# Weight decode sums on VectorE, copies of turned probabilities on ScalarE, in a decay-attention and low-rank MLP kernel

## The chip, the cores and the metric

The kernel runs on one core of one Trainium2 chip. The metric is the device time of an execution in microseconds; the median of several runs is compared. The core has five engines that run side by side and meet at semaphores: TensorE (PE, with its weight loads PEld), VectorE (DVE), ScalarE (ACT), GpSimd (POOL) and SyncE (SP), which here issues nearly all DMAs.

## The reference

Attention over 8 batches x 8 heads, 576 tokens, head size 64, with a causal decay, and then a token mix of rank 32 and a channel MLP on the result:

```python
scores = scale * np.matmul(q, k.transpose(0, 1, 3, 2))
log_f = np.log(np.clip(f, 0.0001, 1.0))
cum = np.cumsum(log_f, axis=-1)
decay = cum[:, :, :, None] - cum[:, :, None, :]
scores = np.where(causal, -1000000000.0, scores + decay)
attn = np.exp(scores - np.max(scores, axis=-1, keepdims=True))
attn = attn / (np.sum(attn, axis=-1, keepdims=True) + 1e-09)
x = heads_to_columns(np.matmul(attn, v))
h = x.transpose(0, 2, 1) @ U @ V
u = x + h.transpose(0, 2, 1)
return u + np.maximum(u @ w_ch1, 0.0) @ w_ch2
```

`w_ch1` is 512 x 2048, `w_ch2` 2048 x 512. U, V and both matrices reach the chip as 64-bit floating-point numbers.

## The kernel before

**Steps and pairs.** The 64 heads are worked on as 32 pairs (four to a batch). A step (`step(t)`) has ten slots. It computes the scores of pair t (S for the four main row blocks of both heads, St for the 64-token tail), turns the probabilities of pair t−1 over on TensorE (T, T_v, Ty) and multiplies them with the values: head 0 of pair t−1 in slot 7 of step t, head 1 in slot 0 of step t+1 (V). Behind that come the rank-32 product (Tt), and after every fourth pair the mix (H, Tu, Tv) and the first part of the MLP (A, B), slipped in between the slots. A score block goes: S on TensorE into a PSUM bank; a row maximum with the mask on VectorE (L365, L391 for the tail), which writes nm; the exponential on ScalarE (L373, L401), which writes P and frees the bank. Each V group ends with its evacuation to xn on VectorE (L520 and L525), which frees the one V area of PSUM that T_v uses too.

**The first six pairs** (p < NF = 6) work in plain float32: the turned probabilities are copied once out of PSUM. `evac` records that copy. In `turn_p` the groups 0 and 2 of each head are copied by ScalarE and group 1 (128x384) by VectorE; in `turn_tail` the two halves of the turned tail (128x256 each) by VectorE. From the seventh pair on (p >= 6) the operands are split into a high and a low part: ScalarE copies the high part (L422), VectorE subtracts to get the low one (L423), whatever engine `evac` was given. Of these pairs GpSimd builds the split operands G of the scores (L309 on POOL, L322, L323), and it also makes the low part of xn for the rank-32 product in every step (L595, L596).

**The weight decode.** Before the seventh pair, fourteen weight units are brought from 64-bit numbers into a high part (h) and a low part (l): units 0, 1, 3, 4, 6, 7 are chunks of w1, unit 2 is U, unit 5 is V, units 8 to 13 are chunks of w2. Each is loaded by SyncE into a staging tile (`load_w`; stg for w1, U, V; a part of the third xn buffer and stg for w2) two or three units ahead, and decoded (`decode_w`, `decode`) at places in the steps that the list DECODES gives: two to three units a step from step 0 to 5, the last in step 7. One decode is eight instructions on one tile: a scaling on ScalarE (L60), bit work on VectorE (L65, L66, L67, L68), the sum of the two parts (L69), the rounding copy to h on ScalarE (L70) and the subtraction that leaves l (L71). L69 and L71 are on `sub`, which is GpSimd for all fourteen units. Each waits for the one ahead of it. A second decode, of the remaining weights at about 710 to 810 us, has `sub=nc.vector` already and is not touched.

**What sets the order.** TensorE's order is written out by hand in the whole attention part. In step 0, and from step 7 on, SyncE's is too. The orders of VectorE, ScalarE and GpSimd (in steps 1 to 6 SyncE's as well) are made by the scheduler when the program is built, so a change of engine reorders what stands around it; pins (`keep_in_program_order`) hold only each decode's first instruction, the w2 loads and the clearing of G. Every engine works its queue strictly in order.

Of the kernel before, what the change touches and what calls it, by code (L numbers as in the profile page):

```python
# [21 lines left out]
P = 128  # L22
# [18 lines left out]
def tile_decay_attention_moe(ctx, tc, qk, v, f, U, V, w1, w2, out):  # L41
    nc = tc.nc
# [8 lines left out]
    def decode(raw, a, h, l, eng, rows=slice(0, 128), keep=False, sub=nc.gpsimd):  # L51

        lo, hi = raw[..., 0].bitcast(U32), raw[..., 1]
        af, gf = a.bitcast(F32), hi.bitcast(F32)
        if eng is nc.scalar:
            first = nc.scalar.mul(af, gf, 2.0**-112)  # L60
        else:
            first = eng.tensor_scalar(af, gf, 2.0**-112, None, op0=ALU.mult)
        if keep:
            tc.keep_in_program_order(first)
        nc.vector.tensor_scalar(hi, hi, -0x80000000, None, op0=ALU.bitwise_and)  # L65
        nc.vector.scalar_tensor_tensor(a, a, 3, hi, op0=ALU.logical_shift_left, op1=ALU.bitwise_or)  # L66
        nc.vector.tensor_scalar(hi, a, -0x800000, None, op0=ALU.bitwise_and)  # L67
        nc.vector.scalar_tensor_tensor(gf, lo, 2.0**-52, gf, op0=ALU.mult, op1=ALU.mult)  # L68
        sub.tensor_tensor(af, af, gf, op=ALU.add)  # L69
        nc.scalar.copy(h, af)  # L70
        sub.tensor_tensor(l[rows], af[rows], h.bitcast(F32)[rows], op=ALU.subtract)  # L71
# [126 lines left out]
    def load_w(u):  # L198
        if u in staged or u >= len(UNITS):
            return  # L200
        kind, fc = UNITS[u]
        n = {"U": (NM + 1) * RK, "V": S}.get(kind, 512)
        if kind == "w2":

            spare = xn[NX - 1].rearrange("p c d -> p (c d)").bitcast(I32)
            if fc % 2:
                raw, a = spare[:, 1536:2560], sb.tile([P, 512], I32, tag="w2a", name=f"stg{u}")
            else:
                raw, a = spare[:, 0:1024], spare[:, 1024:1536]
        else:  # L210
            t = sf.tile([P, 3 * S], I32, tag=("uh", "ul", "hh", "hl")[u % 4], name=f"stg{u}")
            raw, a = t[:, 0 : 2 * n], t[:, 2 * n : 3 * n]
        staged[u] = raw.rearrange("p (n t) -> p n t", t=2), a
        if kind == "w1":
            nc.sync.dma_start(raw, w1_src(fc))
        elif kind == "w2":
            tc.keep_in_program_order(nc.sync.dma_start(raw, w2_src(fc)))
        elif kind == "V":
            for g in range(4):
                nc.sync.dma_start(raw[32 * g : 32 * g + 32], words(V))  # L220
        else:
            r4 = raw.rearrange("p (c r) -> p c r", c=NM + 1)
            nc.sync.dma_start(r4[:, 0:NM], words(U[0:MAIN]).rearrange("(c p) r -> p c r", p=P))
            for g in range(2):
                nc.sync.dma_start(r4[64 * g : 64 * g + 64, NM], words(U[MAIN:S]))

    def decode_w(u):
        load_w(u)
        raw, a = staged.pop(u)
        staged[u] = None  # L230
        kind, fc = UNITS[u]
        if kind == "w1":
            h, l = (x[:, fc].rearrange("p c f -> p (c f)") for x in (w1h, w1l))
        elif kind == "w2":
            h, l = w2h[:, fc], w2l[:, fc]
        elif kind == "V":
            h, l = VV, VV
        else:
            raw = raw.rearrange("p (c r) t -> p c r t", c=NM + 1)
            a = a.rearrange("p (c r) -> p c r", c=NM + 1)  # L240
            h, l = Us[:, :, 0:RK], Us[:, :, RK : 2 * RK]
        decode(raw, a, h, l, nc.scalar, slice(96, 128) if kind == "V" else slice(0, 128), keep=True)
        if u == len(UNITS) - 1:
            nc.gpsimd.memset(xn[NX - 1][64:128, NM, :], 0.0)

# [7 lines left out]
    def defer(phase, fn, slots=1):  # L253
        later.setdefault(now[0] + slots, []).append((phase, fn))
# [53 lines left out]
    def copy(eng, dst, src):  # L308
        return eng.copy(dst, src) if eng is nc.scalar else eng.tensor_copy(dst, src)  # L309
# [105 lines left out]
        nc.vector.reciprocal(z["rv"][:, 0:9], sm[:, 0:9])  # L415
        nc.vector.tensor_copy(z["rv"][0:64, 9:10], z["rv"][64:128, 8:9])

    def evac(dsth, dstl, src, eng=nc.scalar):
        if dstl is None:
            defer(0, lambda: copy(eng, dsth, src))  # L420
            return
        defer(0, lambda: nc.scalar.copy(dsth, src))  # L422
        defer(2, lambda: nc.vector.tensor_tensor(dstl, src, dsth.bitcast(F32), op=ALU.subtract))  # L423

    GRP = (((0, 0), (0, 1), (0, 2), (0, 3)), ((1, 1), (1, 2), (1, 3)), ((2, 2), (2, 3), (3, 3)))
# [1 line left out]
    def turn_p(p, j, g):  # L427
        z = st[p]
        if "PTh" not in z:
            kind = F32 if p < NF else F32R  # L430
            z["PTh"] = sb.tile([P, 2, PTW], kind, tag="PTh", name=f"PTh{p}")
            z["PTl"] = sb.tile([P, 2, PTW], F32R, tag="PTl", name=f"PTl{p}") if p >= NF else None
            z["PT4"] = sb.tile([P, P], kind, tag="PT4", name=f"PT4{p}")
        grp = GRP[g]
        if (j, g) == (0, 2):
            z["tv"] = psV.tile([P, 1024], F32, tag="V", name=f"T{p}_v")
            tp = z["tv"][:, 0:512]
        else:
            tp = psT.tile([P, 512], F32, tag="T", name=f"T{p}_{j}{g}")
        for x, (c, i) in enumerate(grp):  # L440
            nc.tensor.transpose(tp[:, P * x : P * x + P], z["P"][j][i][:, P * c : P * c + P], ident)  # L441

        x = 0
        for c in sorted({c for c, _ in grp}):
            m = sum(1 for cc, _ in grp if cc == c)
            sl = slice(OC[c], OC[c] + P * m)
            low = z["PTl"][:, j, sl] if p >= NF else None
            evac(z["PTh"][:, j, sl], low, tp[:, P * x : P * (x + m)], nc.vector if g == 1 else nc.scalar)
            x += m

    def turn_tail(p):
        z = st[p]
        tp = z["tv"][:, 512:1024]
        for c in range(NM):
            nc.tensor.transpose(tp[:, P * c : P * c + P], z["ptl"][:, P * c : P * c + P], ident)

        tpv = tp.rearrange("p (c j t) -> p j c t", c=NM, j=2)
        for c in range(0, NM, 2):
            o = [(OC[c + y] + MAIN - P * (c + y)) // TAIL for y in range(2)]
            pair = [  # L460
                z[n] and z[n].rearrange("p j (y d) -> p j y d", d=TAIL)[:, :, o[0] : o[1] + 1 : o[1] - o[0]]
                for n in ("PTh", "PTl")
            ]
            evac(pair[0], pair[1], tpv[:, :, c : c + 2], nc.vector)

    def turn_small(pa, px):

# [284 lines left out]
    with tc.manual_schedule(engines=None):  # L752
# [30 lines left out]
        stream(bare, 26)  # L783
        load_w(3)
    decode_w(0)
    mixing = []
    DECODES = [(0, 2), (0, 5), (0, 8), (1, 2), (1, 7), (2, 3), (2, 8), (3, 6), (4, 2), (4, 6), (5, 2), (5, 6), (7, 1)]
# [6 lines left out]
    def step(t):  # L794
# [11 lines left out]
        for s in range(6 + 2 if last else SLOTS):  # L806
# [20 lines left out]
            if (t, s) in DECODES:  # L827
                u = 1 + DECODES.index((t, s))

                steps = [lambda: load_w(u + (3 if u < 6 else 2)), lambda: decode_w(u)]  # L830
                for fn in steps if u < 8 else steps[::-1]:
                    at(6, fn)
# [21 lines left out]
            if pa and s < 3:  # L854
                turn_p(a, 0, s)
# [4 lines left out]
            if pa and s == 5:  # L860
                turn_tail(a)
            if pa and 6 <= s < 9:
                turn_p(a, 1, s - 6)
# [110 lines left out]
    def first(g, u, i):  # L974

        ps = psF.tile([P, 512], F32, tag="F", name=f"Hb{g}_{i}")
        m = 0
        for c in range(NDC):
            for wt_, ut in ((b1h, u[0]), (b1l, u[0]), (b1h, u[1])):
                nc.tensor.matmul(ps, wt_[i][:, c], ut[:, c, 0:MAIN], start=m == 0, stop=m == 3 * NDC - 1)  # L980
                m += 1
        h = hidden(f"{g}_{i}")
        relu(h, ps, slice(0, MAIN))
        return h
# [25 lines left out]
    for i in range(NB // 2):  # L1010
        blocks = []
        for x in range(3):
            if i < 3:
                pair = [hm[:, i, 2 * P * x : 2 * P * x + 2 * P] for hm in homes]
            else:
                k = 6 * (i - 3) + 2 * x
                pair = [more[y // 4][:, 256 * (y % 4) : 256 * (y % 4) + 256] for y in (k, k + 1)]
# [114 lines left out]
    u = cur  # L1132
    ready = []
    with tc.manual_schedule(engines={ET.PE}):
        for n, g in enumerate(order):
# [4 lines left out]
            z = {"g": g, "acc": acc, "po": [None] * NM, "done": [0] * NM}  # L1140
            if n == 0:
                for i in range(NB):
                    h = first(g, u, i)
# [17 lines left out]
            u = un  # L1161
# [50 lines left out]
```

## Time and profile before

| | |
|---|---|
| median of 3 runs | 1255.39 us (1253.97 to 1256.29) |
| the profiled execution's own time | 1257.95 us |
| its span, first to last instruction | 1256.2 us |
| mean granted TensorE clock | 0.989 |
| busy PE / DVE / ACT / POOL | 97% / 69% / 51% / 36% |
| DMA | 125.87 MB, 100 GB/s over the span |

Busy times come from one execution taken by the hardware profiler. A row of a timeline gives the start in us, the time in us, engine, line, operation, tiles (written <- read), their size and a count, and in brackets how long the engine stood idle before it and what released it; "issue" means that the profile shows no releaser. A row of a group gives the least, median and largest time of one instruction in ns and the first and last start. A row of the stage table gives the stage, its length, the busy time of PE, PEld, DVE, ACT and POOL with instruction counts, the granted clock of TensorE (1.00 is full), the share of the DMA engines and GB/s. TensorE's float32 matmuls are recorded as more than one instruction, so counts there are larger than in the program.

### The profile page before, as it was taken

Reading aid. Unit: us, or ns where it says so; the run is one execution under the profiler, and the core shown is the slowest. Engines: PE = TensorE matmul, PEld = TensorE weight load, DVE = VectorE, ACT = ScalarE, POOL = GpSimd, SP = SyncE. Lnnn points to the kernel's source line nnn. Section 1 sums busy time; section 2 is a strip of 40 time slices with the busy share of each in tenths; the row PEclk is TensorE's granted clock in tenths of the full one; section 3 lists DMA queues with packets and bytes.
Section 4 is the critical chain, followed back from the end, with each engine's and each line's share of the span. In section 5 each row is a group of like instructions: output and inputs, shape, how many; then the busy total and the mean of one; then the engine's idle time right before and its main releaser. Section 6 shows DMA issues by size and latency. Waiting matters only on the chain.

```text
span 1256.2 us, 21878 instructions
## 1 busy us (share of the span) xinstructions
PE 1215.8 (97%) x7824; PEld 1074.1 (86%) x7824; DVE 866.6 (69%) x2193; ACT 638.5 (51%) x1717; POOL 456.3 (36%) x403
## 2 busy tenths in 40 slices
PE   8898899999999999999999999989999999999998
PEld 4676798998988998989989888878888888888887
DVE  8776778767778668777777699884554645556453
ACT  5565677867777767778666443332121221212211
POOL 5445455534444444545342000342331513315100
PEclk9798999999999999999999999999999999999999
DMA  7533332632434425326322256110221303213010
GB/s 178 132 106 108 113 104 71 182 96 76 140 94 149 118 75 167 85 71 179 98 74 89 92 175 253 34 68 29 106 85 51 135 9 127 79 56 134 2 34 34
DMA packets 67580, 125.87 MB, mean 100 GB/s; under 512 B 7408, under 2 KB 31984, under 8 KB 65424
## 3 DMA queue, kind: packets, MB, share of 16 engines
q1 hardware_dynamic: 67408, 124.47, 32.4%
q8 instruction: 62, 1.02, 0.4%
q14 instruction: 46, 0.38, 0.1%
q10 hardware_dynamic: 64, 0.00, 0.0%
HBM read 88.65 MB, written 35.78 MB: 99 GB/s over the span
## 4 chain that ended last, share of the span: by engine, by line
PE 81%; DVE 8%; ACT 6%; issue 3%; DMA 2%; SPq 0%; POOL 0%; ACTq 0%; DVEq 0%; POOLq 0%
PE O L994 20%; PE M L1070 16%; PE A L701 10%; PE B L719 9%; PE V L544 5%; PE T L441 3%; PE S L344 3%; PE Hb L980 2%; PE V L516 2%; PE S L345 2%; ACT G L309 1%; ACT P L373 1%; PE Tt L610 1%; PE St L344 1%; PE S L341 1%
## 5 line engine op out<-in xcount | busy, mean ns | idle before, releaser
L1093 DVE TENSOR_TENSOR sum<-M,sum 128x256 f32<-128x256 f32 x280 | 117.6, 422 | 172.2 <-PE M L1070 171.2
L971 ACT ACTIVATE bh<-sum 128x256 fp32r<-128x256 f32 x160 | 66.3, 418 | 258.6 <-DVE sum L1093 258.6
L373 ACT ACTIVATE P<-S,nm 128x128 f32<-128x128 f32 (+3 forms) x256 | 137.3, 537 | 64.8 <-DVE nm L365 52.6
L365 DVE CUSTOM_DVE_ANT_0 S<-S,mask 128x128 f32<-128x128 f32 (+3 forms) x256 | 125.7, 495 | 55.9 <-PE S L345 45.8
L994 PE MATMUL O<-b2h,bh 128*128 128x512 f32 x360 | 142.9, 397 | 0.0
L994 PE MATMUL O<-b2l,bh 128*128 128x512 f32 x360 | 142.2, 395 | 0.0
L994 PE MATMUL O<-b2h,bl 128*128 128x512 f32 x360 | 141.7, 394 | 0.0
L309 POOL CAST G<-qk 64x576 fp32r<-64x576 f32 x52 | 34.6, 666 | 250.3 <-PE St L345 150.8
L701 PE MATMUL A<-uh,w1h 128*128 128x256 f32 (+1 forms) x384 | 120.4, 314 | 2.1 <-DVE hl L705 2.1
L185 POOL TENSOR_TENSOR Tl<-xn,Th 128x512 fp32r<-128x512 f32 x32 | 41.3, 1303 | 202.5 <-PE M L1070 178.9
L701 PE MATMUL A<-uh,w1l 128*128 128x256 f32 (+1 forms) x384 | 113.5, 296 | 0.0
L701 PE MATMUL A<-ul,w1h 128*128 128x256 f32 (+1 forms) x384 | 113.5, 296 | 0.0
L972 DVE SCALAR_TENSOR_TENSOR bl<-sum,bh 128x256 fp32r<-128x256 f32 x160 | 93.2, 587 | 19.6 <-ACT bh L971 18.9
L1053 POOL TENSOR_TENSOR xn<-u 128x512 f32<-128x512 f32 x32 | 43.4, 1379 | 166.9 <-DVE b1l L71 106.4
L719 PE MATMUL B<-w2h,hh 128*128 128x512 f32 x216 | 90.3, 418 | 1.7 <-DVE ost L733 1.0
L441 PE MATMUL T<-ident,P 128*128 128x128 f32 x544 | 87.4, 277 | 0.0
L719 PE MATMUL B<-w2l,hh 128*128 128x512 f32 x216 | 85.0, 394 | 0.0
L719 PE MATMUL B<-w2h,hl 128*128 128x512 f32 x216 | 84.5, 391 | 0.0
L423 DVE TENSOR_TENSOR PTl<-T,PTh 128x512 fp32r<-128x512 f32 (+1 forms) x156 | 79.0, 525 | 6.9 <-ACT PTh L422 6.5
L994 PEld LDWEIGHTS O<-b2l,bh 128*128 128x128 f32 x360 | 67.7, 188 | 16.5
L994 PEld LDWEIGHTS O<-b2h,bl 128*128 128x128 f32 x360 | 68.1, 189 | 11.2
L994 PEld LDWEIGHTS O<-b2h,bh 128*128 128x128 f32 x360 | 68.0, 189 | 10.6
(240 smaller groups left out, 3594.6 us busy)
## 6 DMA issues: line engine op xcount, KB each, us to landing
qk<-in_qk_dram SPq DMA_DIRECT2D x104, 288.0 KB
u<-ud SPq DMA_DIRECT2D x16, 1024.0 KB
sr<-in_w_dram SPq DMA_DIRECT2D x20, 512.0 KB
vr<-in_v_dram SPq DMA_DIRECT2D x32, 256.0 KB
accd<-ost SPq DMA_DIRECT2D x32, 256.0 KB
xn<-accd SPq DMA_DIRECT2D x8, 1024.0 KB
out_dram<-xn SPq DMA_DIRECT2D x32, 256.0 KB
ud<-uh SPq DMA_DIRECT2D x7, 1024.0 KB
```

What stands on the lines that cost most here:

```text
L365: nc.vector.tensor_tensor_reduce(ps[:, :w], ps[:, :w], mask[:, 512 - w : 512], scale=-SCALE, scalar=3.0e38, op0=ALU.add, op1=ALU.min, accu ...
L373: nc.scalar.activation(pt, ps[:, :w], AF.Exp, bias=z["nm"][:, col : col + 1], scale=-1.0, accum_out=z["sm"][:, col : col + 1])
L423: defer(2, lambda: nc.vector.tensor_tensor(dstl, src, dsth.bitcast(F32), op=ALU.subtract))
L441: nc.tensor.transpose(tp[:, P * x : P * x + P], z["P"][j][i][:, P * c : P * c + P], ident)
L544: nc.tensor.matmul(pv[0:m, X0 + lo : X0 + hi], VS[:, c, j, 0:m], z[("PTh", "PTl")[x]][:, j, OC[c] + lo - P * c : OC[c] + hi - P * c], star ...
L701: nc.tensor.matmul(ps[:, :nt], wt[:, fc, c], ut[:, c, sl], start=m == 0, stop=m == 3 * NDC - 1)
L719: nc.tensor.matmul(ps, ht[:, fc, P * x : P * x + P], wt[:, fc], start=fc == 0 and m == 0, stop=fc == NA - 1 and m == 2,)
L971: nc.scalar.activation(hh, src, AF.Relu)
L972: nc.vector.scalar_tensor_tensor(hl, src, 0.0, hh.bitcast(F32), op0=ALU.max, op1=ALU.subtract)
L994: nc.tensor.matmul(po, ht[:, P * x : P * x + P], wt_[i], start=k == 0 and m == 0, stop=k == NB - 1 and m == 2)
L1070: nc.tensor.matmul(ps, a[x][:, c], b[y][:, c], start=m == 0, stop=m == 5)
L1093: nc.vector.tensor_tensor(dst, ps, other, op=ALU.add)
```

## The change

Two edits. First, `decode_w` hands `sub` on: the sum (L69) and the subtraction (L71) are on VectorE for units 1 to 13, and stay on GpSimd for unit 0. Second, `evac` has no engine any more: every copy of turned probabilities is on ScalarE, so in the first six pairs the copies of group 1 and of the tail move from VectorE to ScalarE. From the seventh pair on `evac` records the same as before.

```diff
-        decode(raw, a, h, l, nc.scalar, slice(96, 128) if kind == "V" else slice(0, 128), keep=True)
+        decode(raw, a, h, l, nc.scalar, slice(96, 128) if kind == "V" else slice(0, 128), keep=True, sub=nc.vector if u else nc.gpsimd)
...
-    def evac(dsth, dstl, src, eng=nc.scalar):
+    def evac(dsth, dstl, src):
+        defer(0, lambda: nc.scalar.copy(dsth, src))
         if dstl is None:
-            defer(0, lambda: copy(eng, dsth, src))
             return
-        defer(0, lambda: nc.scalar.copy(dsth, src))
         defer(2, lambda: nc.vector.tensor_tensor(dstl, src, dsth.bitcast(F32), op=ALU.subtract))
...
-            evac(z["PTh"][:, j, sl], low, tp[:, P * x : P * (x + m)], nc.vector if g == 1 else nc.scalar)
+            evac(z["PTh"][:, j, sl], low, tp[:, P * x : P * (x + m)])
...
-            evac(pair[0], pair[1], tpv[:, :, c : c + 2], nc.vector)
+            evac(pair[0], pair[1], tpv[:, :, c : c + 2])
```

In the changed kernel lines from 418 on have numbers one lower, and the copies of the first six pairs stand at L419 (before at L309, in a helper).

TensorE's order is the same, row for row. VectorE has 26 sums more and 24 copies fewer; GpSimd the 26 sums fewer. Two places of the new order matter to what follows.

The first is VectorE at the turn from step 1 to step 2, where unit 5 (V, stg_271) meets the evacuation of head 1 of pair 0 (V_1_480 into xn). Before:

```order
L65 TENSOR_SCALAR stg_271<-stg_271 128x576
L66 SCALAR_TENSOR_TENSOR stg_271<-stg_271 128x576
L414 TENSOR_SCALAR sm_322<-sm_322 128x9
L67 TENSOR_SCALAR stg_271<-stg_271 128x576
L415 RECIPROCAL rv_547<-sm_322 128x9
L520 TENSOR_TENSOR xn_105<-V_1_480,rv_379 128x4x64
L525 TENSOR_SCALAR xn_105<-V_1_480,rv_379 64x64
L68 SCALAR_TENSOR_TENSOR stg_271<-stg_271 128x576
```

The same place in the changed kernel (stg_211 and stg_247 are the units 3 and 4 of w1):

```order
L71 TENSOR_TENSOR w1l<-stg_211,w1h 128x512
L68 SCALAR_TENSOR_TENSOR stg_247<-stg_247 128x512
L65 TENSOR_SCALAR stg_271<-stg_271 128x576
L519 TENSOR_TENSOR xn_105<-V_1_480,rv_379 128x4x64
L524 TENSOR_SCALAR xn_105<-V_1_480,rv_379 64x64
L414 TENSOR_SCALAR sm_322<-sm_322 128x9
L69 TENSOR_TENSOR stg_247<-stg_247 128x512
L365 ISA S_01_513,nm_469<-S_01_513,mask 128x256
```

The evacuation stood four instructions behind L65 of unit V and now stands directly behind it; a sum and a subtraction of other units have come in between the score reductions.

The second is the copy of the turned tail of pair 1 (PTh_496 from T_v, 128x2x2x64, twice) in step 2. On VectorE before:

```order
L65 TENSOR_SCALAR stg_301<-stg_301 128x512
L66 SCALAR_TENSOR_TENSOR stg_301<-stg_301 128x512
L391 ISA St_1_564,nm_469<-St_1_564,mask,nm_469 128x288
L391 ISA nm_469 128x1
L309 COPY PTh_496<-T_v 128x2x2x64 x2
L67 TENSOR_SCALAR stg_301<-stg_301 128x512
L365 ISA S_10_586,nm_469<-S_10_586,mask 128x128
```

On ScalarE in the changed kernel:

```order
L60 ACTIVATE stg_301<-stg_301 128x512
L479 COPY PT_497<-Ty_None 64x128
L373 ACTIVATE P_03_545,sm_470<-S_03_542,nm_469 128x512
L419 COPY PTh_496<-T_v 128x2x2x64 x2
L419 COPY PTh_496<-T_10_581 128x512
L419 COPY PTh_496<-T_11_594 128x384
L401 ACTIVATE Ptl_574,sm_470<-St_0_552,nm_469 128x288
L401 ACTIVATE Ptl_574,sm_470<-St_1_564,nm_469 128x288
```

The tail copies stood behind two decode instructions and the tail's second reduction on VectorE; on ScalarE they stand behind an exponential, and ahead of the tail's two exponentials (L401).

## Prediction

> **What bounds the kernel now.** I read the page's header and its parts on engines and on the chain that ended last, then the busy time by stage, then the timelines of single engines.
>
> ```profile
> span 1256.2 us, 21878 instructions
> PE 1215.8 (97%) x7824; PEld 1074.1 (86%) x7824; DVE 866.6 (69%) x2193; ACT 638.5 (51%) x1717; POOL 456.3 (36%) x403
> PE 81%; DVE 8%; ACT 6%; issue 3%; DMA 2%; SPq 0%; POOL 0%; ACTq 0%; DVEq 0%; POOLq 0%
> ```
>
> TensorE is the bound: 97% busy, 81% of the chain. The change touches only the first seven steps, so the question is how far TensorE is held up there. The stage table (us, PE, PEld, DVE, ACT, POOL, granted clock) says:
>
> ```profile
> 0.00:60.00 60.00, 49.00 (x242) 32.93 (x243) 50.86 (x128) 32.43 (x91) 29.55 (x40) 0.90 0.63 163
> 60.00:120.00 60.00, 55.14 (x374) 43.39 (x373) 44.66 (x126) 35.65 (x112) 29.20 (x31) 0.95 0.39 108
> 120.00:180.00 60.00, 56.40 (x402) 50.86 (x402) 41.88 (x118) 40.48 (x114) 31.50 (x29) 0.94 0.32 93
> 180.00:240.00 60.00, 59.27 (x446) 54.78 (x445) 48.80 (x142) 48.08 (x138) 30.51 (x28) 1.00 0.51 145
> ```
>
> Until 180 us TensorE idles 11.0 + 4.9 + 3.6 us and its granted clock is below 1; afterwards it is full at full clock. So whatever is won or lost before 180 us moves everything behind it by as much. In TensorE's timeline (start, us, instruction, idle before it and releaser) these places matter:
>
> ```profile
> 29.13 3.44 PE L516 MATMUL V<-vr,PTh 128*128 128x64 f32 x28 [1.31 <-issue]
> 46.01 0.52 PE L441 MATMUL T_v<-ident,P 128*128 128x128 f32 x3 [2.64 <-DVE xn L525]
> 53.33 3.65 PE L516 MATMUL V<-vr,PTh 128*128 128x64 f32 x28 [1.55 <-issue]
> 62.43 2.95 PE L516 MATMUL V<-vr,PTh 128*128 128x64 f32 x28
> 72.57 2.95 PE L516 MATMUL V<-vr,PTh 128*128 128x64 f32 x28
> 78.46 2.95 PE L516 MATMUL V<-vr,PTh 128*128 128x64 f32 x28
> 90.38 3.29 PE L516 MATMUL V<-vr,PTh 128*128 128x64 f32 x28 [1.18 <-issue]
> 97.89 2.95 PE L516 MATMUL V<-vr,PTh 128*128 128x64 f32 x28
> 118.69 0.30 PE L344 MATMUL S<-G 128*128 128x128 f32 x1 [2.07 <-ACT P L373]
> ```
>
> Each V group multiplies the turned probabilities of one head; it cannot start before their last copy. "issue" names no releaser, but VectorE's timeline does:
>
> ```profile
> 42.49 0.46 DVE L65 TENSOR_SCALAR stg<-stg 128x576 int32<-128x576 int32 x1 [2.47 <-ACT stg L60]
> 43.79 1.49 DVE L67 TENSOR_SCALAR stg<-stg 128x576 int32<-128x576 int32 x1
> 45.32 0.36 DVE L520 TENSOR_TENSOR xn<-V,rv 128x256 f32<-128x256 f32 x1
> 50.24 1.88 DVE L66 SCALAR_TENSOR_TENSOR stg<-stg 128x512 int32<-128x512 int32 x1
> 52.49 0.75 DVE L309 COPY PTh<-T_v 128x256 f32<-128x256 f32 x2
> 89.53 0.74 DVE L309 COPY PTh<-T_v 128x256 f32<-128x256 f32 x2
> ```
>
> The copies of the turned tail end at 53.24 and 90.27, and V starts at 53.33 and 90.38. They stand in VectorE's queue behind decode instructions, and those are stretched while GpSimd adds:
>
> ```profile
> 43.66 1.30 POOL L71 TENSOR_TENSOR w1l<-stg,w1h 128x512 fp32r<-128x512 f32 x1 [3.18 <-ACT w1h L70]
> 50.17 1.41 POOL L71 TENSOR_TENSOR VV<-stg,VV 32x576 fp32r<-32x576 f32 x1 [0.24 <-ACT VV L70]
> 114.05 1.73 POOL L71 TENSOR_TENSOR w2l<-stg,w2h 128x512 fp32r<-128x512 f32 x1
> ```
>
> L67 at 43.79 takes 1.49 us beside the first, L66 at 50.24 takes 1.88 beside the second.
>
> A gap also costs clock. Two stages behind V's gaps, and the 2.64 us wait itself:
>
> ```profile
> 44.00:46.00 2.00, 0.00 (x0) 0.02 (x1) 2.00 (x5) 0.52 (x2) 0.96 (x1) 1.00 0.60 168
> 55.00:62.50 7.50, 7.50 (x37) 5.40 (x36) 5.27 (x12) 2.78 (x8) 3.97 (x3) 0.54 0.01 2
> 93.00:96.50 3.50, 3.50 (x19) 2.55 (x18) 2.78 (x5) 0.18 (x1) 2.40 (x2) 0.52 0.24 89
> ```
>
> From V of head 0 to V of head 1 TensorE has the same work in steps 2, 3 and 4: it takes 78.46 − 72.57 = 5.89 us undisturbed, 62.43 − 53.33 = 9.10 behind the 1.55 us gap, 97.89 − 90.38 = 7.51 behind the 1.18 us one.
>
> **The change, part by part.** Prices first:
>
> ```profile
> L69 DVE TENSOR_TENSOR xn<-xn,sr x20: 674/682/691, 716.0 to 807.7; 128x512 f32<-128x512 f32 x20
> L309 DVE COPY PTh<-T x12: 543/552/555, 22.9 to 138.3; 128x384 f32<-128x384 f32 x12
> L309 DVE COPY PTh<-T_v x12: 409/414/421, 28.3 to 135.7; 128x256 f32<-128x256 f32 x12
> L422 ACT CAST PTh<-T x156: 271/491/623, 148.9 to 699.2; 128x512 fp32r<-128x512 f32 x52, 128x384 fp32r<-128x384 f32 x52, 128x256 fp32r<-128x256 f32 x26, 128x128 fp32r<-128x128 f32 x26
> L422 ACT CAST PTh<-T_v x104: 268/373/401, 152.0 to 693.4; 128x256 fp32r<-128x256 f32 x78, 128x128 fp32r<-128x128 f32 x26
> ```
>
> *Load.* Thirteen units bring two sums each: 26 x 0.68 = 17.7 us at most on VectorE (U is smaller). It loses 12 x 0.55 + 12 x 0.41 = 11.6 us of copies, so it has some 6 us more work, in 180 us in which it idles 180 − (50.9 + 44.7 + 41.9) = 42.5. ScalarE gets 12 x 0.49 + 12 x 0.37 = 10.3 us (medians of rows of mixed widths), where it idles 71. Neither is full; what counts is the order at the places above.
>
> *The wait for T_v at 46.01.* The first place of the order shows it: the evacuation of V (L520) now stands directly behind L65 of unit V. L65 ends at 42.49 + 0.46 = 42.95, L520 began at 45.32, so TensorE goes on 2.37 us earlier, unless the DMA that L65 waits for lands later. SyncE's issue of that load waited for U's low half on GpSimd and now waits for it on VectorE; earlier loads in SyncE's order hold it just as long. Gain **2.37** (bounds 0 and 2.64).
>
> *The gap at 53.33.* The tail copies stand on ScalarE, behind the transposes' end and two short instructions. Here ScalarE had nothing to do:
>
> ```profile
> 50.73 0.59 ACT L309 COPY PTh<-T 128x512 f32<-128x512 f32 x1
> 52.66 0.50 ACT L401 ACTIVATE Ptl<-St,nm 128x288 f32<-128x288 f32 x1 [1.34 <-DVE nm L391]
> ```
>
> Two copies of 0.37 fit; V no longer waits: **1.55**. Without the gap I expect the full clock behind it: 9.10 − 5.89 = **3.21**.
>
> *The gap at 90.38*, likewise: 1.18 + (7.51 − 5.89) = **2.80**.
>
> *The gap at 29.13* also closes, but I count nothing: the load that both engines await next is not moved.
>
> ```profile
> 32.49 0.66 ACT L60 ACTIVATE stg<-stg 128x512 f32<-128x512 f32 x1 [4.02 <-DMA stg<-in_w_dram]
> 41.67 0.73 ACT L60 ACTIVATE stg<-stg 128x576 f32<-128x576 f32 x1 [2.95 <-DMA stg<-in_V_dram]
> ```
>
> ScalarE stands at 28.5 to 32.5 and 38.7 to 41.7 for weights, with the exponentials that free score banks behind it. Bounds 0 and 1.31.
>
> *The gap at 118.69* comes from a run of decode instructions on VectorE ahead of a score reduction, beside GpSimd's split of pair 6's operands, which stays, and w2's subtraction above, which goes. In its place a 0.68 us subtraction of an earlier unit stands in that run. I count 0; bounds −0.68 and +2.07.
>
> *New waits.* In steps 5 and 6 the tail copies stand ahead of the tail's exponentials, which free the score bank that TensorE waits for:
>
> ```profile
> 109.44 1.18 PE L341 MATMUL S<-qk 128*128 128x128 f32 x4 [0.58 <-ACT Ptl L401]
> ```
>
> That wait grows by about one copy, 0.4. In step 2 the third and fourth score reductions stand behind L71 and L69: 0.3 estimated. The last unit (step 7) puts 2 x 0.68 on VectorE between reductions: 0.4 estimated, bounds 0 and 1.36. Together **−1.1**. GpSimd's clearing of G is no longer held by w2's subtraction and moves to step 3, where it can stretch L65 and L67 of another unit instead of the one it stretched in step 4; SyncE then issues G's decay rows ahead of a w2 load. I count 0 for both.
>
> [...]
>
> Sum: 2.37 + 1.55 + 3.21 + 2.80 − 1.1 = **8.8 us** less. The profiled execution's own time was 1257.95 (span 1256.2), so it would be 1249.1; that execution lies 2.6 above the median 1255.39 of the three runs, so for the median I forecast **1246.6**.
>
> **The rivals.**
>
> *The clock does not follow the gaps* (0.20). For it: a 2.64 us standstill at 44 to 46 left the clock at 1.00, so the length of a gap alone doesn't set it. Against it: both shorter gaps, each followed by V groups, were followed by half clock. Then only waits go: 2.37 + 1.55 + 1.18 − 1.1 = 4.0, 1251.4. [...]
>
> *More goes* (0.17): the gap at 29.13 and the one at 118.69 with them, 1.31 + 2.07, and about as much clock as at 90.38, 1.62: 13.8 in all, 1241.6.
>
> *Nothing moves* (0.13): the weights' DMA landings and the operands of pair 6 set the pace of the first 120 us, and an earlier TensorE only waits longer there: 1255.4.
>
> *Slower* (0.12): VectorE takes over GpSimd's waits for ScalarE's casts, with score reductions queued behind them.
>
> ```profile
> POOL w1l L71 <- ACT w1h L70: 9.5, 5, 3.2
> POOL Us L71 <- ACT Us L70: 3.5, 1, 3.5
> ```
>
> GpSimd stood there 13.0 us, with nothing else to do. If VectorE stood as long with TensorE behind it, the time would be 1246.6 + 13.0 = 1259.6; it decides from 8.8 us on. Against it: the order puts other work between each sum and its cast's user.
>
> **How the numbers follow.** The forecast has 0.38. A measurement of this kernel tells about 0.2% (2.5 us) from no change. Faster by more than that, under 1252.9: the forecast, "more goes", and most of "the clock does not follow", 0.38 + 0.17 + 0.17 = 0.72. Within: the rest of the latter and "nothing moves", 0.03 + 0.13 = 0.16. Slower: 0.12. The range reaches down past 1241.6 with both open gaps to 1240, and up over "nothing moves" to 1256.5; outside are the slower case and a small tail below, under 0.2.
>
> **What would show it.** Right: in the changed profile V of head 0 starts without a gap in steps 2 and 4, T_v's wait in step 2 is under 0.5 us, the stage from V of head 0 to V of head 1 in step 2 takes about 5.9 us at full clock, and TensorE reaches pair 6 some 9 us earlier. Wrong: the waits go but half-clock stages of the same length stand elsewhere (the first rival), ScalarE's wait for weights grows by what TensorE won (the third), or VectorE shows waits for ScalarE's casts at L71 ahead of score reductions with TensorE idle (the last).

## The result, and the profile after

| | before | after |
|---|---|---|
| median | 1254.68 us (4 runs, 1253.20 to 1256.29) | 1242.78 us (4 runs, 1242.18 to 1244.96) |
| profiled execution's own time | 1257.95 us | 1242.59 us |
| mean granted TensorE clock, profiled execution | 0.989 | 0.999 |

The changed kernel takes 0.9901 of the time before (95% interval 0.9884 to 0.9918): 11.9 us less at the medians, where 8.8 were forecast. The two profiled executions lie 15.4 us apart; why that is more than is usual comes out of the experiments. The page of the changed kernel (span; busy times; the chain by engine):

```profile
span 1240.8 us, 21851 instructions
PE 1204.0 (97%) x7824; PEld 1066.0 (86%) x7824; DVE 861.3 (69%) x2195; ACT 645.5 (52%) x1741; POOL 424.5 (34%) x377
PE 82%; DVE 8%; ACT 6%; issue 2%; DMA 2%; SPq 0%; ACTq 0%; POOL 0%; DVEq 0%; POOLq 0%
```

Over the whole span the shares hardly move: "issue" goes from 3% to 2% of the chain, PE from 81% to 82%. The stage table (us, PE, PEld, DVE, ACT, POOL, granted clock, DMA share, GB/s) shows where:

```profile
0.00:60.00 60.00, 51.75 (x300) 36.16 (x301) 52.53 (x150) 40.06 (x117) 17.28 (x31) 1.00 0.65 173
60.00:120.00 60.00, 54.35 (x394) 43.91 (x393) 47.75 (x132) 43.02 (x128) 18.50 (x24) 1.00 0.39 110
120.00:180.00 60.00, 57.92 (x447) 53.80 (x446) 45.35 (x130) 43.94 (x131) 29.54 (x25) 1.00 0.41 113
```

The clock is full up to 180 us, where it was 0.90, 0.95 and 0.94. TensorE's timeline after, at the places quoted of before:

```profile
27.64 2.95 PE L515 MATMUL V<-vr,PTh 128*128 128x64 f32 x28
...
31.86 0.91 PE L341 MATMUL S<-qk 128*128 128x384 f32 x2 [1.01 <-ACT Ptl L401]
...
41.06 0.52 PE L440 MATMUL T_v<-ident,P 128*128 128x128 f32 x3 [1.84 <-DVE sm L414]
...
46.81 2.95 PE L515 MATMUL V<-vr,PTh 128*128 128x64 f32 x28
...
52.70 2.95 PE L515 MATMUL V<-vr,PTh 128*128 128x64 f32 x28
...
78.86 2.95 PE L515 MATMUL V<-vr,PTh 128*128 128x64 f32 x28
...
84.74 2.95 PE L515 MATMUL V<-vr,PTh 128*128 128x64 f32 x28
...
96.44 1.18 PE L341 MATMUL S<-qk 128*128 128x128 f32 x4 [0.79 <-ACT Ptl L401]
...
105.58 0.30 PE L344 MATMUL S<-G 128*128 128x128 f32 x1 [1.96 <-ACT P L373]
```

All three gaps ahead of V are gone, and from V of head 0 to V of head 1 (V to V from here on) it takes 5.89 us in step 2 (52.70 − 46.81) and 5.88 in step 4, as forecast. Behind V of step 1 a wait of 1.01 us stands, for an exponential of the tail that ScalarE has queued behind a load (30.66 below). The wait at T_v has not gone: 1.84 us, with L414 named as releaser. L414 isn't what T_v needs. ScalarE and, in the second fence, VectorE show what is:

```profile
30.66 0.66 ACT L60 ACTIVATE stg<-stg 128x512 f32<-128x512 f32 x1 [1.93 <-DMA stg<-in_w_dram]
...
39.19 0.71 ACT L60 ACTIVATE stg<-stg 128x576 f32<-128x576 f32 x1 [3.79 <-DMA stg<-in_V_dram]
...
45.63 0.64 ACT L419 COPY PTh<-T_v 128x256 f32<-128x256 f32 x2
...
77.64 0.65 ACT L419 COPY PTh<-T_v 128x256 f32<-128x256 f32 x2 [0.61 <-PE T_v L454]
```

```profile
39.94 0.46 DVE L65 TENSOR_SCALAR stg<-stg 128x576 int32<-128x576 int32 x1 [2.90 <-ACT stg L60]
40.31 0.42 DVE L519 TENSOR_TENSOR xn<-V,rv 128x256 f32<-128x256 f32 x1
```

The evacuation L519 now follows L65 directly, as the order said it would, and L65 stands in the queue until unit V's weights have landed. ScalarE's L60 starts 0.10 us after the last of the transfers has landed (39.09 us here, 41.57 before), so its start tells the landing: 39.19 us against 41.67 before. From there to T_v it takes 41.06 − 39.19 = 1.87 us, before 46.01 − 41.67 = 4.34.

### The profile page after: what moved, and what is told of

It reads as the page before. It is cut to its first block, busy times and chain, and to the rows that moved or that the text cites. A ratio compares the mean times of both kernels' runs of the same rounds, so it can differ in the third digit from the quotient of the medians.

```text
span 1240.8 us, 21851 instructions
## 1 busy us (share of the span) xinstructions
PE 1204.0 (97%) x7824; PEld 1066.0 (86%) x7824; DVE 861.3 (69%) x2195; ACT 645.5 (52%) x1741; POOL 424.5 (34%) x377
## 4 chain that ended last, share of the span: by engine, by line
PE 82%; DVE 8%; ACT 6%; issue 2%; DMA 2%; SPq 0%; ACTq 0%; POOL 0%; DVEq 0%; POOLq 0%
PE O L993 20%; PE M L1069 16%; PE A L700 10%; PE B L718 9%; PE V L543 5%; PE T L440 3%; PE S L344 3%; PE Hb L979 2%; PE V L515 2%; PE S L345 2%; ACT P L373 1%; ACT G L309 1%; PE Tt L609 1%; PE St L344 1%; PE S L341 1%
## 5 line engine op out<-in xcount | busy, mean ns | idle before, releaser
L309 POOL CAST G<-qk 64x576 fp32r<-64x576 f32 x52 | 34.9, 671 | 250.1 <-PE St L345 149.5
L322 POOL TENSOR_TENSOR G<-qk,G 64x576 fp32r<-64x576 f32 x52 | 74.4, 1431 | 15.6 <-ACT G L309 6.2
L993 PEld LDWEIGHTS O<-b2h,bl 128*128 128x128 f32 x360 | 68.2, 189 | 11.2
```

Source lines behind the costliest of these rows:

```text
L322: pin(el.tensor_tensor(g[oth, 2, cols], k[oth], gf[oth, 2, cols], op=ALU.subtract))
L993: nc.tensor.matmul(po, ht[:, P * x : P * x + P], wt_[i], start=k == 0 and m == 0, stop=k == NB - 1 and m == 2)
```

## The experiments

Beside the time, each run gives its mean granted clock. In the profiles the granted clock stands at 1.00 or at 0.50, so the time at half clock is 2 x (1 − clock) x span. A straight line through all 122 runs, with a height for each kernel and one slope for all, gives **0.32 us (±0.05) lost for each us at half clock**; the height is the time that the kernel would take at full clock throughout (±0.8 to 1.4). That parts what waits cost from what the clock costs:

| kernel | runs | median us | half clock, mean us | at full clock, us |
|---|---|---|---|---|
| before (with the second profile of it) | 60 | 1255.8 | 24.2 | 1247.7 |
| after (both sets) | 10 | 1244.3 | 11.2 | 1240.8 |
| sums only | 5 | 1249.0 | 11.0 | 1245.2 |
| copies only | 4 | 1244.9 | 11.2 | 1241.1 |
| before, gaps filled | 10 | 1252.4 | 12.3 | 1248.4 |
| tail copies only | 5 | 1248.3 | 18.9 | 1242.0 |
| group copies only | 6 | 1249.7 | 17.5 | 1244.4 |
| after, unit V later | 6 | 1244.6 | 14.1 | 1239.7 |
| after, two more units later (both sets) | 11 | 1241.0 | 8.6 | 1238.9 |
| after, pair 6's gap filled | 5 | 1243.1 | 6.5 | 1240.3 |

The figures behind ± are 95% intervals. So the change takes 6.9 us (±1.0) of waits and 0.32 x (24.2 − 11.2) = 4.2 us of half clock.

**Sums only.** Theory: the copies' place in VectorE's queue makes the gaps, and half clock follows them. Rival A: GpSimd's stretching of the decode instructions ahead of them makes the copies late.

```diff
-        decode(raw, a, h, l, nc.scalar, ..., keep=True)
+        decode(raw, a, h, l, nc.scalar, ..., keep=True, sub=nc.vector if u else nc.gpsimd)
```

> Before, with the sums of units 1 to 13 on VectorE and every copy of turned probabilities left where it was. Main theory (the tail copies' place on VectorE sets the idle time ahead of V, and half clock follows it): the gaps ahead of V in steps 1, 2 and 4 stay, and with subtractions added in the same queue they are no shorter than 1.31, 1.55 and 1.18 us; clock stays below 1; the time is at best 2 us below before, from the T_v wait alone, or a few us above it. Rival A (GpSimd stretches VectorE's decode instructions, and that stretch is what makes the tail copies late): the gaps close or halve, and the kernel shows most of the whole change's 11.9 us, a time of 1243 to 1247. Rival B (the clock does not follow gaps): only waits differ, within 3 us of before.

1248.96 us; ratio 0.9940 (0.9927 to 0.9953). Three rows of its timeline of TensorE and two of VectorE's:

```profile
29.39 3.02 PE L516 MATMUL V<-vr,PTh 128*128 128x64 f32 x28 [1.56 <-issue]
...
50.93 3.03 PE L516 MATMUL V<-vr,PTh 128*128 128x64 f32 x28 [0.68 <-PE T L441]
...
83.97 3.02 PE L516 MATMUL V<-vr,PTh 128*128 128x64 f32 x28 [0.76 <-PE T L441]
```

```profile
49.31 0.42 DVE L65 TENSOR_SCALAR stg<-stg 128x512 int32<-128x512 int32 x1
...
50.08 0.75 DVE L309 COPY PTh<-T_v 128x256 f32<-128x256 f32 x2
```

In step 2 nothing of GpSimd runs beside the decode instructions (0.00 us busy from 48 to 52 us), L65 takes 0.42 us ahead of the tail copies, and these come sooner. The gaps fall from 1.55 to 0.68 us in step 2 and from 1.18 to 0.76 in step 4, though the sums have joined the same queue; in step 1 the gap grows, from 1.31 to 1.56. My expectation that none would be shorter was wrong in two of three places. Rival A's halving happened in step 2 alone, and its time of 1243 to 1247 is not reached. The scheduler's new order also puts L66 behind the tail copies in step 2, so this run doesn't tell the stretch from the order.

**Copies only.** The other half of the change:

```diff
-        decode(raw, a, h, l, nc.scalar, ..., keep=True, sub=nc.vector if u else nc.gpsimd)
+        decode(raw, a, h, l, nc.scalar, ..., keep=True)
```

> The changed kernel with decode's sums back on GpSimd: of the change, only the copies on ScalarE. Main theory: no gap ahead of V in steps 1, 2 and 4, full clock behind them; the T_v wait in step 2 stays near 2.6 us, and the 2.07 us wait for a score reduction in step 5 may grow with its half clock. Time 1245 to 1248, most of the gain. Rival A (GpSimd's stretching matters): the gain is small, 1250 or above. Rival B (clock does not follow gaps): 1250 to 1252, about 3 us below before, with half-clock stretches elsewhere.

1244.92 us; ratio 0.9908 (0.9895 to 0.9921), that of the whole change. TensorE's timeline:

```profile
41.52 0.52 PE L440 MATMUL T_v<-ident,P 128*128 128x128 f32 x3 [2.45 <-DVE xn L524]
47.12 3.05 PE L515 MATMUL V<-vr,PTh 128*128 128x64 f32 x28 [0.23 <-ACT PTh L419]
```

The main theory holds, 0.1 us below its range of times and but for a gap of 0.23 us in step 2; the wait at T_v stays, as expected. Once the copies are moved, the sums add nothing that these runs can tell (1241.1 against 1240.8 at full clock, the same half clock): the two halves work on the same gaps, and their gains don't add up. From unit V's landing (38.61) to V of head 0 in step 2 it takes 8.51 us here and 7.62 in the changed kernel; the 0.9 us that the sums seem to give there is within the uncertainty of the heights.

**Before, gaps filled.** TensorE is kept busy in the gaps, and no wait is made shorter:

```diff
+        if p in (0, 1, 3) and (j, g) == (1, 1):
+            for _ in range(22):
+                nc.tensor.matmul(tp[:, 384:512], blank[:, 0:P], blank[:, 0:P], start=True, stop=True)
```

> Before, with 22 extra bf16 matmuls of 128 columns on TensorE after the second group of transposes of head 1 in steps 1, 2 and 4, written to columns that nothing reads: TensorE is busy while V of head 0 waits for its copies, and no wait is shorter than before. Main theory (idle time just ahead of V makes the half clock): the stages behind V in steps 2 and 4 run at full clock; V to V takes 5.9 us there instead of 9.1 and 7.5, and 2.5 us more is won behind V of step 1; about 7 us in all less what the matmuls hold up, a time of 1247 to 1250. Rival B (the clock does not follow these gaps): the time is that of before or up to 3 us above it, and V to V stays near 9.1 and 7.5 us.

1252.41 us; ratio 0.9973 (0.9960 to 0.9985). V of heads 0 and 1 in steps 2 and 4:

```profile
54.45 3.00 PE L519 MATMUL V<-vr,PTh 128*128 128x64 f32 x28
...
60.39 2.95 PE L519 MATMUL V<-vr,PTh 128*128 128x64 f32 x28
...
88.30 3.03 PE L519 MATMUL V<-vr,PTh 128*128 128x64 f32 x28
...
94.26 2.95 PE L519 MATMUL V<-vr,PTh 128*128 128x64 f32 x28
```

V to V takes 5.94 and 5.96 us where it took 9.10 and 7.51. Half clock falls from 24.2 to 12.3 us a run at the waits of before (1248.4 against 1247.7): the clock does follow idle TensorE, and the rival by which it doesn't falls. The mean over the runs shows it; V to V in one profile would not, as the next run tells. The gain is smaller than I expected; in its profile half clock stands at 39.6 to 43.0 and 46.4 to 49.8 us instead.

**Before again.** The same program, profiled a second time:

> The kernel before, unchanged, profiled once more. If the half-clock stretches are set by the kernel's own order, they stand again near 31 to 38, 55 to 62, 93 to 96 and 120 to 127 us, with V-to-V stages near 9.1 us in step 2 and 7.5 us in step 4, and the weights' transfers land near 32.5 and 41.7 us. If they fall by chance, they stand elsewhere or are missing, and the stages last 5.9 us.

1255.09 us. TensorE's timeline:

```profile
29.30 3.02 PE L516 MATMUL V<-vr,PTh 128*128 128x64 f32 x28 [1.32 <-issue]
...
52.20 4.74 PE L516 MATMUL V<-vr,PTh 128*128 128x64 f32 x28 [1.54 <-issue]
...
61.28 2.95 PE L516 MATMUL V<-vr,PTh 128*128 128x64 f32 x28
...
89.20 3.03 PE L516 MATMUL V<-vr,PTh 128*128 128x64 f32 x28 [1.17 <-issue]
...
95.16 2.95 PE L516 MATMUL V<-vr,PTh 128*128 128x64 f32 x28
```

The gaps are the same to 0.01 us, the half clock is not: behind the gap of step 2 it stands again (61.28 − 52.20 = 9.08), behind those of steps 1 and 4 it is missing (95.16 − 89.20 = 5.96). The two loads land at 31.55 and 40.55 us, 0.9 and 1.1 us earlier than in the first profile. So the same gap was followed by half clock in one execution and not in the next: that of step 2 both times, those of steps 1 and 4 once in two. This is a good part of why the profiled pair shows 15.4 us: that execution of before caught all four stretches, that of after none before 800 us.

**Which copies.** Before, with one kind of copies moved, first the tail's, then that of group 1:

```diff
-            evac(pair[0], pair[1], tpv[:, :, c : c + 2], nc.vector)
+            evac(pair[0], pair[1], tpv[:, :, c : c + 2])
```

> Before, with only the six pairs' tail copies (the last two ahead of each V) moved from VectorE to ScalarE; the copies of the second groups of transposes and all sums stay. Main theory (it is the tail copies, last in VectorE's queue ahead of V, that make the gaps and bring on the half clock): the gaps of 1.31, 1.55 and 1.18 us go, half clock behind them goes, the time is 1245 to 1247, nearly that of all copies moved (1244.9). Rival (any relief of VectorE does it): the gain is about that of moving only the other copies. Rival B (clock independent of gaps): 1251 to 1252.

```diff
-            evac(..., tp[:, P * x : P * (x + m)], nc.vector if g == 1 else nc.scalar)
+            evac(..., tp[:, P * x : P * (x + m)])
```

> Before, with only the copies of the second groups of transposes (128x384) moved to ScalarE in the six pairs; the tail copies stay on VectorE. Main theory: the tail copies still stand behind stretched decode instructions, so the gaps ahead of V in steps 1, 2 and 4 stay above 1 us and the time is within 3 us of before, 1253 to 1256. Rival (any relief of VectorE does it): the gaps shrink to half or less and the time is 1248 to 1250.

1248.26 us, ratio 0.9933 (0.9917 to 0.9948), and 1249.72, ratio 0.9948 (0.9933 to 0.9964). The first is 1.3 us above what I expected: with the tail copies moved no gap is left ahead of V of head 0 in steps 1, 2 and 4, but a wait for the tail's exponential shows in step 1, and half clock from 33.7 us on (first fence). ScalarE had that exponential queued behind L60, where it stood 2.70 us for a load (second fence); it is the load that the prediction named there, not the copies. With the group copies moved, three gaps are left (third fence):

```profile
33.73 2.50 PE L341 MATMUL S<-qk 128*128 128x512 f32 x4 [1.69 <-ACT Ptl L401]
...
36.03 3.47 PE L516 MATMUL V<-vr,PTh 128*128 128x64 f32 x28
```

```profile
31.83 0.66 ACT L60 ACTIVATE stg<-stg 128x512 f32<-128x512 f32 x1 [2.70 <-DMA stg<-in_w_dram]
```

```profile
29.06 3.02 PE L516 MATMUL V<-vr,PTh 128*128 128x64 f32 x28 [1.23 <-issue]
...
50.53 3.02 PE L516 MATMUL V<-vr,PTh 128*128 128x64 f32 x28 [0.73 <-PE T L441]
...
83.22 3.02 PE L516 MATMUL V<-vr,PTh 128*128 128x64 f32 x28 [0.41 <-PE T L441]
```

At full clock the tail copies give 5.7 us and the group copies 3.3, together with nothing else 6.6. My expectation for the second was wrong in two of three gaps and by 3 us of time; its rival, any relief of VectorE, is what happened in steps 2 and 4, and the time lies in the rival's range. Fewer copies ahead in VectorE's queue help the tail copies too. At full clock the tail copies are the larger part, not the only one.

**Unit V later.** Is the wait at T_v due to L65 standing in the queue for its weights?

```diff
-    DECODES = [..., (1, 2), (1, 7), (2, 3), (2, 8), ...]
+    DECODES = [..., (1, 2), (2, 1), (2, 5), (2, 8), ...]
```

> The changed kernel itself once more, beside the two below. It should give 1242 to 1245 us with granted clocks of 0.995 to 0.999, all gaps ahead of V gone in steps 1, 2 and 4, and about 1.8 us of wait for V's evacuation ahead of T_v in step 2.

> The changed kernel with the decode of unit V issued after the evacuation of V in step 2 (and the unit behind it two places later). Main theory: the 1.84 us wait at T_v in step 2 comes from VectorE standing in the first instruction of unit V's decode until its weights have landed, with the evacuation queued behind it; with the decode behind the evacuation that wait goes, and the time falls by up to 1.8 us, to 1241 to 1242. Rival: TensorE then waits for the same landing or for the decoded unit a little later, and the time is that of the changed kernel within 0.5 us.

1244.91 us (clocks 0.991 to 0.997, lower than expected, and a wait of 1.37 us at T_v, not 1.8) and 1244.55. The wait at T_v is gone from the profile, and the stage from V of head 1 in step 1 to V of head 0 in step 2 takes 45.09 − 33.94 = 11.15 us, where the two profiles of the changed kernel have 12.79 and 12.33:

```profile
33.94 2.95 PE L515 MATMUL V<-vr,PTh 128*128 128x64 f32 x28
...
45.09 3.02 PE L515 MATMUL V<-vr,PTh 128*128 128x64 f32 x28
```

So the cause is L65's stand: the wait is gone in the two profiles of the next kernel too, which has the same edit, though there V of head 0 in step 2 waits 0.84 us for the values' load and 0.57 us for its copies instead. The time is that of the rival, within 0.5 us of the changed kernel: the 1.1 us that the edit gives at full clock is within the uncertainty of these runs (±1.2), and these runs had more half clock (14.1 us against 11.2).

**Two more units later.** The wait ahead of pair 6's first scores at 105.58:

```diff
-    DECODES = [..., (1, 2), (1, 7), (2, 3), ..., (5, 2), (5, 6), (7, 1)]
+    DECODES = [..., (1, 2), (2, 1), (2, 5), ..., (5, 4), (6, 6), (7, 1)]
```

> As the kernel before it, with two more units moved in the order: one from the middle to later in step 5, one from step 5 to the end of step 6. Aim: the score reductions of head 1 in step 5, which now stand behind some seven decode instructions on VectorE, come free, so the 1.96 us wait ahead of pair 6's first scores at 105.6 us goes. Main theory: 2 us less again, 1239 to 1240. Rival: the operands of pair 6, which GpSimd splits at 98 to 102 us, or the weights decoded later set the end there, and nothing is gained, 1241 to 1243.

> The kernel with unit V and two more units decoded later, once more, to see whether its lead on the changed kernel stands: 1240.5 to 1243 us by the first look, a wait of well under 1 us ahead of pair 6's first scores, and no half clock near 108 us. If its lead was chance, 1243 to 1245.

1242.04 us, ratio to before 0.9901 (0.9876 to 0.9926), and 1240.50, ratio 0.9880 (0.9858 to 0.9902). The first lies in the range of its rival, by which nothing is gained, though 2.5 us below unit V later beside it; the second is at the lower end of the range expected for it. The 1.96 us wait is gone in both profiles; the first of them:

```profile
98.95 1.18 PE L341 MATMUL S<-qk 128*128 128x128 f32 x4 [1.28 <-ACT Ptl L401]
...
106.22 3.00 PE L515 MATMUL V<-vr,PTh 128*128 128x64 f32 x28
```

From V of head 0 in step 5 (100.30) to V of head 1 it takes 106.22 − 100.30 = 5.92 us, in the second profile too, against 8.03 (105.82 − 97.79) in the changed kernel; 0.5 of it is given back in the wait for Ptl (1.28 against 0.79). Over both sets it is the fastest kernel here: 1.9 us (±1.1) below the changed one at full clock.

**What the clock goes by.** Every half-clock stretch in the first 160 us of the profiles is 3.41 or 6.83 us long. Cut before's stage table at its boundaries (same columns):

```profile
41.77:45.18 3.41, 1.60 (x9) 0.88 (x7) 2.65 (x4) 2.65 (x7) 1.30 (x1) 1.00 0.86 207
...
52.01:55.42 3.41, 2.09 (x19) 2.12 (x20) 3.28 (x13) 2.63 (x9) 0.07 (x1) 1.00 0.03 8
55.42:58.83 3.41, 3.41 (x16) 2.34 (x16) 3.27 (x5) 0.63 (x2) 2.62 (x2) 0.50 0.00 0
```

Each stretch is wholly at 1.00 or at 0.50. TensorE's 1.60 us of 3.41 in the first were transposes and scores, and the clock stayed; its 2.09 us in the second quoted were all V (64 columns wide), and the clock fell. I counted V's time at one half and everything else in full, over some 500 such stretches at full clock between 10 and 150 us in 13 profiles: the 13 with the least counted time, up to 1.30 us, were all followed by half clock; of five between 1.38 and 1.52 three were; above that none. With V at 0.4 or 0.6 the best bound leaves two or three stretches on the wrong side, with V in full, which is plain busy time, eleven. The weight and the bound were chosen to fit the first eleven of these profiles, so this is a description, not a mechanism that is shown, and I put it to one new test, filling pair 6's gap in the changed kernel:

```diff
+                if (p, s) == (6, 0):
+                    for _ in range(30):
+                        nc.tensor.matmul(st[4]["spare"], blank[:, 0:P], blank[:, 0:P], start=True, stop=True)
```

> The changed kernel with 30 extra bf16 matmuls of 128 columns on TensorE ahead of pair 6's first scores, written to columns that nothing reads: TensorE is busy in the 1.96 us for which it waits there. Rule under test, from the profiles so far: the clock is set anew every 3.41 us, and halves when in that stretch the time in matmuls, with those of V counted at one half, was under about 1.5 us. By it no half clock can begin between 100 and 112 us (a stretch with V all through counts 1.7), where five of the earlier profiles have one of 6.8 us; the stage from V of head 1 in step 5 to V of head 0 in step 6 takes 16.5 to 16.8 us, not 18.5 to 19.3. Time: that of the changed kernel or up to 2 us below. Rival (the clock falls by chance, or with the length of a wait alone): half clock near 108 us as often as before, that stage up to 19.3 us, time that of the changed kernel or more.

1243.09 us; ratio 0.9898 (0.9880 to 0.9917). First the second profile of the changed kernel at that place, cut the same way, then that of the filled one:

```profile
104.00:107.41 3.41, 1.44 (x10) 0.87 (x8) 3.36 (x11) 1.46 (x5) 0.00 (x0) 1.00 0.47 126
107.41:110.83 3.42, 3.42 (x19) 3.30 (x17) 1.23 (x6) 1.88 (x4) 1.40 (x1) 0.50 0.00 0
```

```profile
102.87:106.28 3.41, 3.41 (x37) 2.52 (x37) 3.41 (x9) 1.05 (x4) 0.98 (x1) 1.00 0.64 165
106.28:109.70 3.42, 3.14 (x34) 2.99 (x31) 3.00 (x12) 2.83 (x7) 0.00 (x0) 1.00 0.04 8
```

No half clock began there. From V of head 1 in step 5 to V of head 0 in step 6 it takes 124.01 − 107.48 = 16.53 us, as expected, against 126.10 − 106.82 = 19.28 in the second profile of the changed kernel. One profile is not enough, since the first of the changed kernel, with the gap open, has 16.53 as well (122.35 − 105.82); what speaks for the rule is that half clock falls from 11.2 to 6.5 us a run, over five runs against ten. The test agrees with the rule; it doesn't tell the weight of V from another one.

## Why the prediction was right, and where it was off

- **The time.** 1242.78 us is within the range, and nearer to the rival "more goes" (1241.6) than to the forecast of 1246.6. Of the two places by which that rival differs, the gap at 29.13 closed and the one at 118.69 stayed. TensorE reaches pair 6 13.1 us earlier in the first pair of profiles (118.69 to 105.58) and 9.4 in the second (115.99 to 106.57), where some 9 was the sign.
- **The gap at 53.33 (1.55) and the gap at 90.38 (1.18): right.** Both are gone, by the copies. ScalarE makes the tail copies at 45.63 and 77.64, ahead of V at 46.81 and 78.86. From V of head 1 in step 3 to V of head 0 in step 4 the gain is 11.92 − 10.14 = 1.78 us, 0.6 more than the gap. That the gaps come from the tail copies' place alone was too narrow: the sums alone and the group copies alone shorten those of steps 2 and 4 with the tail copies left on VectorE.
- **The wait for T_v (2.37): right.** From unit V's landing to T_v it takes 4.34 us in both profiles of before and 1.87 in both of the changed kernel, 2.47 less. To V of head 0 in step 2, with the gap of 1.55, it is 4.0 less (11.66 and 7.62). The wait itself fell only from 2.64 to 1.84, since TensorE reached T_v 4.15 us earlier and the landing came only 2.48 earlier. So the sign that I gave, a wait under 0.5 us, was the wrong one: a wait that ends with a load's landing is priced from the landing.
- **The gap at 29.13 (0): right that the load is awaited next, wrong that its time is fixed.** The gap closed and V of head 0 starts 1.49 us earlier (27.64). But TensorE still waits for unit V's landing in step 2, so what is kept of the 1.49 is what the landing moved: 41.67 and 40.55 us in the two profiles of before, 39.19 and 40.16 in two of the changed kernel, 40.84 in the one with pair 6's gap filled. That is about 1 us on the mean and 1.7 between executions with the changed order, so its size is not settled. SyncE issues the last part of V at 36.1 and 35.3 us before and at 34.6, 34.7 and 35.0 after, which fits buffers that come free earlier; no run tried it alone.
- **New waits (−1.1): too much.** The wait for Ptl in step 5 grew from 0.58 to 0.79, not by 0.4; with the tail copies alone moved it is 0.79 too. From V of head 1 in step 4 to V of head 0 in step 5 it takes 13.05 instead of 12.90 us.
- **The clock (3.21 + 1.62 = 4.83): near in sum, 4.2 measured over the runs, but in part by luck.** Half clock isn't tied to a gap: the 1.62 behind the gap of step 4 is missing in the second profile of before. How often it comes went with the gaps: 24.2 us a run with them, 12.3 with them filled. Of the rivals, "the clock does not follow the gaps" was worth its 0.20 by the rows that I had; the 2.64 us wait that spoke for it left transposes and scores in its stretch (1.60 us, just above the bound of the fitted rule), the shorter gaps left V.
- **The gap at 118.69 (0): right.** 1.96 us is left of 2.07, and it goes only when the decode instructions on VectorE are moved away.
- **Waits:** forecast 2.37 + 1.55 + 1.18 − 1.1 = 4.0, measured 6.9 (±1.0). Of the 2.9 between, about 1 is the landing, 0.6 the rest of step 4, and about 1 the new waits that didn't come.
- **The slower rival** needed VectorE to stand at L71 for ScalarE's casts. It doesn't: all five groups of L71 on VectorE between 14 and 160 us (busy us, mean ns, idle us ahead) show 0.0 us of idle time, the largest of them here.

```profile
L71 DVE TENSOR_TENSOR w1l<-stg,w1h 128x512 fp32r<-128x512 f32 x5 | 3.4, 684 | 0.0
```

## What to carry over

When two edits remove the same wait, price each alone: here the copies gave the whole gain as far as these runs can tell, and the sums, good for 7 us by themselves, added 0.3 us (±1.4) at full clock. An engine that stands in the first instruction of a prefetched task holds whatever the scheduler has put behind it, so place such a task behind the work that frees a buffer: VectorE stood 2.90 us ahead of unit V's L65 with the evacuation behind it, and with that unit later the 1.84 us wait at T_v was gone. And where a wait ends with a load's landing, price the change from the landing to the instruction that waits, and don't take the landing itself as fixed: unit V's moved by up to 1.7 us between executions with the changed order.

## What the runs showed of the hardware that was not expected

- Between two changes of the granted clock there is always a whole number of 3.413 us in the traces of before and after: one or two at half clock, 5 to 207 at full clock. Counted back from a change, these boundaries lie 0.81 us behind the span's start in before and 3.06 in after, so their place against the program differs between executions; 60 runs of the kernel before took 1250.2 to 1259.1 us, at clocks from 0.995 to 0.986. Half clock also came behind a stretch with little idle time: 2.78 us busy of 3.41, nearly all V (copies only, same columns as above).

```profile
105.67:109.08 3.41, 2.78 (x25) 2.74 (x26) 2.17 (x8) 2.81 (x7) 2.29 (x4) 1.00 0.00 0
109.08:112.49 3.41, 3.41 (x19) 2.98 (x18) 1.28 (x4) 1.57 (x4) 2.58 (x2) 0.50 0.26 78
```

- A us at half clock costs 0.32 us on the mean over the runs; with TensorE busy throughout, a clock of 0.50 would cost 0.50 (an estimate from the granted clock alone). Behind the gap of step 2, where TensorE is busy throughout, 6.83 us of it cost 9.10 − 5.89 = 3.21 us, 0.47 for each. Elsewhere TensorE may have waited for part of that time at full clock too; no run tried this.
- In step 2 the decode instruction that stood beside GpSimd's subtraction for unit V was the one stretched: in before L66 took 1.88 us beside it; with the group copies moved L66 takes 0.69, behind it, and L65, 0.42 us when alone (sums only), takes 1.60 beside that subtraction, in which GpSimd is busy until 48.32. No run shows what makes it so.

```profile
47.00 1.60 DVE L65 TENSOR_SCALAR stg<-stg 128x512 int32<-128x512 int32 x1
48.63 0.69 DVE L66 SCALAR_TENSOR_TENSOR stg<-stg 128x512 int32<-128x512 int32 x1
```
